# Fourier mixer, ELU FFN and top-1 MoE in one kernel: the shuffles between transform stages moved to DRAM, the last stage respaced

## The chip, the cores and the metric

One core of one Trainium2 chip runs the whole program. The metric is the device time of one execution in microseconds (us), the median of several runs; lower is better. Times on the trace are counted from the span's start.

## The reference, cut to what matters

```python
def _attn_ref(x, w_r, w_i, b_r, b_i):          # x: 8 x 3072 x 256
    X = np.fft.rfft(x, axis=1)
    Yr = X.real @ w_r - X.imag @ w_i + b_r
    Yi = X.real @ w_i + X.imag @ w_r + b_i
    Yr, Yi = softshrink(Yr, 0.01), softshrink(Yi, 0.01)
    return np.fft.irfft(Yr + 1j * Yi, n=3072, axis=1)
def _moe_ref(x, w_in, w_out):                  # 256 -> 2048 -> 256, ELU
    return elu(x @ w_in) @ w_out
def _moe2_ref(x, expert_emb, tau, w1, w2):     # 8 experts, 256 -> 1024 -> 256
    e = argmax of cosine(x, expert_emb) / tau, gate = its softmax value
    return gate * (relu(x @ w1[e]) @ w2[e])
```

`_attn_ref`, `_moe_ref` and `_moe2_ref` follow one another over 24576 tokens.

## The kernel before, in words

**The transform.** For each of 8 batches the length-3072 transform is done in stages, each number held as a high and a low float16 half, so that each product is three matmuls. Stage A (`unit_a`, L168, 16 steps per batch, each with a `split_x` of the input into halves) transforms over 96; stage B (`unit_b`, L198, 24 units) over 32; M (`unit_m` and `unit_m2`, L227 and L258) is the complex 256 x 256 mixing with bias and soft threshold; D (`unit_d`, L268) and E (`unit_e`, L284, 8 blocks of two halves) are the inverse over 32 and over 96. E writes `yT`, the input of one FFN block of 384 tokens.

**The shuffles.** Between A and B, and between D and E, the index that lies on the partitions changes. Both are done by DMA from SBUF to SBUF. A step of A writes two pieces (L191) of 96 KB, from 96 partitions to 4 partitions of `b_in`; in batch 0, six of these go through POOL's queue and the others through SP's. A unit of D writes 128 KB from 128 partitions to 4 partitions of `e_in` (L282). `b_in` and `e_in` hold a whole batch each. B reads all partitions of `b_in`, so its first unit needs the last step of A; E needs the last unit of D in the same way.

**The weights.** `w_in` and `w_out` arrive as float64. Sixteen pieces of 512 KB (`conv_load`, into `raw`, three buffers) are turned into float32 by three integer instructions of DVE (`conv_a` L319, `conv_a2` L328, `conv_b` L334) and split by `conv_c` (ACT, and POOL or DVE). These 64 items stand in the list `fill`; `hook` puts the next one into the program wherever `credit` allows.

**Batch 0** runs alone at the front (L653 to L709): A with some of the conversions (from step `CA`), `CG` items right after it, then B, M, D with the others, one after the other in a loop of 32 turns: turn i issues B of unit i, M of i-2, the second half of M of i-4 and D of i-7. Then the two halves of E's block 0, and the FFN of batch 0 starts.

**Batches 1 to 7** are woven into the FFN of the batch before. The FFN of one batch has NS = 128 steps (8 blocks of 16), each with `ffn1` (L485) and a later `ffn2` (L511). `plan` (L993 to L1013) is a list of (due step, unit), written by hand and sorted: E of the batch's other blocks early, A of the next batch from step 4.25 on, 3.2 steps apart, B from step 57 on, 2.57 steps apart, with M 1.4, its second half 2.3 and D 3.6 steps behind each B; E of the next batch's blocks 0 and 1 from NS-5 on. What is due is issued twice per step. Every engine and DMA queue works in the order of issue.

SP's queue carries the loads of x, both shuffles, the loads of expert weights (`wexp_load`, L434 and L437) and, from `wexp_split`, the write of the split weights to DRAM (L465), which waits for POOL. After batch 7 the routed expert stage follows.

Of the kernel before, what the change touches and what calls it, by code (L numbers as in the profile page):

```python
# [11 lines left out]
F16 = mybir.dt.float16  # L12
F32 = mybir.dt.float32
# [26 lines left out]
XP = 2  # L40
CA, CG, CN, CV = 8, 10, 24, 18
CD = (1, 2, 3, 5, 6, 7)
# [8 lines left out]
def kernel(  # L51
# [25 lines left out]
    keep = ctx.enter_context(tc.tile_pool(name="keep", bufs=1))  # L77
    rows_d = dram.tile([NROW, RW // 2], I32, name="rows_d")
    wexp_d = [dram.tile([NE * 128, 4096], F16, name=f"wexp{i}_d") for i in range(2)]

# [21 lines left out]
    def pool1(name, bufs):  # L102
        return ph1.enter_context(tc.tile_pool(name=name, bufs=bufs))

    spc = pool1("spc", 1)
    big = pool1("big", 1)
    xp = pool1("xp", XP)
    xs = pool1("xs", 3)
    ao = pool1("ao", 3)
    sb = pool1("sb", 3)  # L110
# [39 lines left out]
    def load_x(b, i):  # L150
        src = x[b].rearrange("(n m) c -> n m c", m=N2)[:, 4 * i : 4 * i + 4, :]
        if b == 0:
            if i == 0:
                xpc[0] = big.tile([96, N2, D], F32, tag="e_in", name="x_0")
            t = xpc[0][:, 4 * i : 4 * i + 4, :]
        else:
            t = xp.tile([N1, 4, D], F32, tag="xpc", name="xpc")
        sp.dma_start(out=t, in_=src)
        xpc[b, i] = t
# [8 lines left out]
    def unit_a(b, g):  # L168
        t = xsp.pop((b, g))
        ps = spec_ps()  # L170
        po = ps[:96, :]
        for n, (i, j) in enumerate(((0, 0), (0, 1), (1, 0))):
            pe.matmul(
                po,
                lhsT=f_sb[:, i, :],
                rhs=t[:, j].rearrange("p n c -> p (n c)"),
                start=n == 0,
                stop=n == 2,
            )
        if b or g % 2 == 0:  # L180
            a = ao.tile([96, 2, 2, D], F16, tag="ao", name="ao")
        else:
            a = pre.tile([96, 2, 2, D], F16, tag="ao", name="ao", bufs=5)
        po2 = po.rearrange("p (n c) -> p n c", n=2)
        copy_hi(a[:, :, 0, :], po2, 2.0**-13)
        copy_lo(a[:, :, 1, :], po2, 2.0**-13, a[:, :, 0, :])
        if g == 0:
            b_in[b] = big.tile([128, NJ, 2 * D], F16, tag="b_in", name="b_in")
        for n in range(2):
            n2 = 2 * g + n  # L190
            (sp if b or not n or g % 2 == 0 or g > 12 else pool).dma_start(  # L191
                out=b_in[b][4 * n2 : 4 * n2 + 4, :, :],
                in_=a[:, n].rearrange("p h c -> p (h c)"),
            )

    s_t = {}
    m_t = {}
    def unit_b(b, j):  # L198
        ps = spec_ps()
        for cc in range(2):  # L200
            for n, (h, i) in enumerate(((0, 0), (0, 1), (1, 0))):
                pe.matmul(
                    ps[:, cc * 128 : (cc + 1) * 128],
                    lhsT=b_in[b][:, j, h * D + cc * 128 : h * D + (cc + 1) * 128],
                    rhs=t_sb[:, j, i, :],
                    start=n == 0,
                    stop=n == 2,
                )
# [59 lines left out]
    def unit_d(b, j):  # L268
# [10 lines left out]
        copy_lo(d[:, 1], ps[:, 0:D], 2.0**-12, d[:, 0])  # L279
        if j == 0:  # L280
            e_in[b] = big.tile([96, N2, 2 * D], F16, tag="e_in", name="e_in")
        sp.dma_start(out=e_in[b][4 * j : 4 * j + 4, :, :], in_=d.rearrange("p h c -> p (h c)"))  # L282

    def unit_e(b, blk, cc):  # L284
# [4 lines left out]
        for m in range(4):  # L289
            m2 = 4 * blk + m  # L290
            for n, (h, i) in enumerate(((0, 0), (0, 1), (1, 0))):
                pe.matmul(
                    ps[:, m * 96 : (m + 1) * 96],
                    lhsT=e_in[b][:, m2, h * D + cc * 128 : h * D + (cc + 1) * 128],
                    rhs=e_sb[:, i, :],
                    start=n == 0,
                    stop=n == 2,
                )
# [144 lines left out]
    def wexp_split(c):  # L443
# [3 lines left out]
        if r < 4:  # L447
            cc, q = divmod(r, 2)
            o = wp.tile([128, 2, 512], F16, tag="wh", name="wh", bufs=1)
            ov = o  # L450
# [3 lines left out]
        else:  # L454
            f = 2 * (r - 4)
            o = wp.tile([128, 2, 512], F16, tag="wh", name="wh", bufs=1)
            ov = o.rearrange("p a b -> p (a b)")
# [158 lines left out]
    sp.dma_start(out=f_sb, in_=c_f)  # L616
    for k in range(8):
        load_x(0, k)
    dve.memset(half, 0.5)
# [8 lines left out]
    dve.tensor_copy(base, eoff)  # L628
    with tc.tile_pool(name="pre", bufs=1, side="right") as pre:
        wm = [pre.tile([128, 512], F32, tag=f"wm{ri}", name=f"wm{ri}") for ri in range(2)]  # L630
        emb_sb = pre.tile([NE, D], F32, name="emb_sb")
        conv_load(order[0], pool)
        first = [
# [22 lines left out]
        for i in range(16):  # L656
            step_a(0, i)
            if i % 2:
                first.pop(0)()
            if i in (5, 9):  # L660
                conv_load(order[i // 4])
            if i >= CA:
                credit[0] = 1
                hook()
        sp.dma_start(out=emb_sb, in_=emb)
# [21 lines left out]
        for i in range(NJ + 8):  # L687
# [7 lines left out]
            if 0 <= i - 7 < NJ:  # L695
                unit_d(0, i - 7)
            if i == 0:
                sp.dma_start(out=d_sb, in_=c_d)
            if i == 1:
# [3 lines left out]
            if i >= CV:  # L703
                step_v()
        credit[0] = len(fill)
        hook(len(fill))
# [5 lines left out]
    tp = ctx.enter_context(tc.tile_pool(name="tp", bufs=2, side="right", reuse_waits="tile"))  # L712
    xo = ctx.enter_context(tc.tile_pool(name="xo", bufs=1, side="right", reuse_waits="tile"))
    rt = ctx.enter_context(tc.tile_pool(name="rt", bufs=2, side="right", reuse_waits="tile"))
# [277 lines left out]
    for b in range(B):  # L992
        plan = []  # L993
        for blk, at in zip(range(1, NBLK), (0, 1, 9, 20, 30, 40, 50)):
            if blk > 1 or b == 0:
                for n, u in enumerate(units_e(b, blk)):
                    plan.append((at + 1.5 * n, u))
        if b + 1 < B:
# [3 lines left out]
            for i in range(16):  # L1002
                plan.append((4.25 + 3.2 * i, lambda i=i: step_a(b + 1, i)))
            for j in range(NJ):
                p = 57 + (NS - 12 - 57) * j / (NJ - 1)
                plan.append((p, lambda j=j: unit_b(b + 1, j)))
                plan.append((p + 1.4 + 0.6 * (j in (0, NJ - 1)), lambda j=j: unit_m(b + 1, j)))
                plan.append((p + 2.3, lambda j=j: unit_m2(b + 1, j)))
                plan.append((p + 3.6, lambda j=j: unit_d(b + 1, j)))
            for blk in range(2):  # L1010
                for n, u in enumerate(units_e(b + 1, blk)):
                    plan.append((NS - 5 + 2 * blk + n, u))
        plan.sort(key=lambda p: p[0])  # L1013
# [163 lines left out]
```

## Time and profile before

| | |
|---|---|
| median of 3 runs | 3925.5 us (3922.7 to 3927.98) |
| profiled execution | 3916.23 us, of which span 3914.1 us |
| busy share of the span | PE 94%, PEld 75%, DVE 65%, ACT 58%, POOL 31% |
| SP's hardware DMA queue | 145.66 MB, 21.8% of 16 engines' span |
| HBM read, written | 285.37 MB, 70.03 MB |
| issues of the first shuffle | 250 on SP, 6 on POOL, 96 KB each |
| issues of the second shuffle | 192 on SP, 128 KB each |

In the rows further down, PE is TensorE, PEld its weight load, DVE VectorE, ACT ScalarE, POOL GpSimd, SPq the DMA queue of SyncE. A line of waits names the waiting instruction, what released it, the total, how often and the longest. A line of a timeline gives start, length, engine, line and operation, and in square brackets how long the engine sat idle just before and what ended that. L92 and L95 are the helpers that write the high and the low half.

### The profile page before, as it was taken

The numbers are of one execution on the slowest core, as the hardware profiler recorded it, in microseconds if no ns is written. First come the engines' busy times: TensorE is split into PE (matmuls) and PEld (weight loads), VectorE is DVE, ScalarE is ACT, GpSimd is POOL, SyncE is SP. The second block draws the span as 40 slices with busy tenths as digits, with TensorE's granted clock in tenths as the row PEclk, the third lists the DMA queues.
The fourth block names the chain that finished last, engine by engine and source line by source line (L and its number), as shares of the span: only waits on it lengthen the run. The fifth ranks groups of instructions, "written<-read, shape, count | busy, mean of one in ns | idle before, by whom it ended". The sixth has DMA issues, their size and how long they took to land. (4 is left out here: it accounts for less than half of the span.)

```text
span 3914.1 us, 81873 instructions
## 1 busy us (share of the span) xinstructions
PE 3697.7 (94%) x32108; PEld 2930.5 (75%) x32108; DVE 2551.1 (65%) x5647; ACT 2267.9 (58%) x4749; POOL 1215.7 (31%) x1529
## 2 busy tenths in 40 slices
PE   3699999999999999999999999999999999999998
PEld 2577777777777777777777777777788899999997
DVE  4676767767677777767677776766665555555554
ACT  3586677668667766866876686677732222222221
POOL 2412223223222222322322232233234444344443
PEclk6899999999999999999999999999999999999999
DMA  6342233224223322422332242210234345533332
GB/s 158 79 68 40 37 60 62 38 43 76 39 38 60 60 37 44 76 38 38 61 60 37 45 77 37 39 46 31 72 97 125 105 115 166 156 77 94 102 90 64
DMA packets 274220, 272.72 MB, mean 70 GB/s; under 512 B 169091, under 2 KB 235354, under 8 KB 265512
## 3 DMA queue, kind: packets, MB, share of 16 engines
q1 hardware_dynamic: 221944, 145.66, 21.8%
q0 software_dynamic: 51888, 121.83, 9.8%
q8 instruction: 251, 4.11, 0.5%
q14 instruction: 137, 1.12, 0.1%
HBM read 285.37 MB, written 70.03 MB: 91 GB/s over the span
## 5 line engine op out<-in xcount | busy, mean ns | idle before, releaser
L511 PE MATMUL ps_a<-wout,ghl 128*128 128x264 f16 x9216 | 1200.3, 276 | 6.6 <-DVE ghl L95 6.1
L485 PE MATMUL ps_h<-yT,win 128*128 128x384 f16 x6144 | 1167.4, 326 | 6.2 <-DVE do L95 3.4
L511 PEld LDWEIGHTS <-ghl 128*128 128x128 f16 x9216 | 890.0, 98 | 209.7 <-DVE ghl L95 11.2
L501 DVE SCALAR_TENSOR_TENSOR g<-e,ps_h 128x384 f32<-128x384 f32 x1024 | 564.7, 552 | 570.7 <-ACT e L498 567.7
L485 PEld LDWEIGHTS <-win 128*128 128x128 f16 x6144 | 596.1, 98 | 314.6 <-issue 10.3
L497 ACT ACTIVATE e<-ps_h 128x384 f32<-128x384 f32 x1024 | 494.0, 482 | 371.7 <-PE ps_h L485 358.6
L913 ACT ACTIVATE r<-ps_h 128x512 f32<-128x512 f32 (+1 forms) x440 | 244.7, 556 | 796.1 <-PE ps_h L907 773.4
L498 ACT ACTIVATE e<-e,top 128x384 f32<-128x384 f32 x1024 | 629.8, 615 | 33.2
L95 DVE SCALAR_TENSOR_TENSOR ghl<-g,ghl 128x768 f16<-128x768 f32 x512 | 510.4, 997 | 85.6 <-ACT ghl L92 85.6
L928 PE MATMUL ps_a<-wbuf,g 128*128 128x256 f16 x4776 | 554.7, 273 | 2.5 <-DVE g L915 1.4
L907 PE MATMUL ps_h<-xt,wbuf 128*128 128x256 f16 (+1 forms) x5280 | 555.5, 262 | 0.0
L907 PEld LDWEIGHTS <-wbuf 128*128 128x128 f16 x5280 | 477.7, 98 | 49.3
L928 PEld LDWEIGHTS <-g 128*128 128x128 f16 x4776 | 464.9, 98 | 57.3 <-DVE g L915 2.5
L606 POOL DMA_INDIRECT rows_d<-row,pi x192 | 203.2, 1059 | 747.8 <-DMA rows_d<-row,pi 309.0
L92 ACT ACTIVATE ghl<-g 128x768 f16<-128x768 f32 x512 | 423.5, 827 | 0.6 <-DVE g L501 0.6
L946 POOL DMA_INDIRECT out_dram<-o,mt x199 | 208.4, 1047 | 518.6 <-DVE o L938 303.4
L914 DVE CAST g<-r 128x512 f16<-128x512 f32 (+1 forms) x440 | 178.5, 406 | 284.2 <-ACT r L913 281.9
L601 POOL COPY row<-gt 128x1 f32<-128x1 f32 x192 | 26.9, 179 | 1083.8 <-DVE gt L597 1083.8
L915 DVE TENSOR_TENSOR g<-r,g 128x512 f16<-128x512 f32 (+1 forms) x440 | 283.0, 643 | 15.1
L241 PE MATMUL ps_h<-wmix,s_t 128*128 128x256 f16 x2106 | 269.5, 274 | 10.4 <-DVE s_t L95 6.4
L241 PEld LDWEIGHTS <-s_t 128*128 128x128 f16 x2256 | 218.8, 99 | 66.1 <-DVE s_t L95 14.0
L938 DVE TENSOR_SCALAR o<-ps_a,mt 128x256 f32<-128x256 f32 x199 | 96.3, 484 | 176.1 <-PE ps_a L928 170.5
(178 smaller groups left out, 3397.7 us busy)
## 6 DMA issues: line engine op xcount, KB each, us to landing
e_in<-do SPq DMA_DIRECT2D x192, 128.0 KB
b_in<-ao SPq DMA_DIRECT2D x250, 96.0 KB
xpc<-in_x_dram SPq DMA_DIRECT2D x56, 384.0 KB
wl<-in_moe_w_dram SPq DMA_DIRECT2D x64, 256.0 KB
wexp_d<-wh SPq DMA_DIRECT2D x64, 256.0 KB
raw<-in_moe_w_in_dram SPq DMA_DIRECT2D x8, 512.0 KB
raw<-in_moe_w_out_dram SPq DMA_DIRECT2D x7, 512.0 KB
out_dram<-o,mt POOLq DMA_INDIRECT x199
```

Source lines behind the costliest of these rows:

```text
L92: act.activation(out=o, in_=i, func=AF.Copy, scale=k)
L95: dve.scalar_tensor_tensor(out=o, in0=i, scalar=k, in1=hi, op0=ALU.mult, op1=ALU.subtract)
L241: pe.matmul(ps[:, 0:D], lhsT=st, rhs=wmix[:, ri, i, cc, :], start=n == 0, stop=n == 11)
L485: pe.matmul(ps[:, 0:BLK], lhsT=win[:, i, cc, f * 128 : (f + 1) * 128], rhs=y[:, h, cc, :], start=n == 0, stop=n == 5,)
L497: act.activation(out=e, in_=ps[:, 0:BLK], func=AF.Exp, scale=2.0**-19)
L498: act.activation(out=e, in_=e, func=AF.Relu, scale=-(2.0**19), bias=top)
L501: dve.scalar_tensor_tensor(out=g, in0=e, scalar=-1.0, in1=ps[:, 0:BLK], op0=ALU.mult, op1=ALU.max)
L511: pe.matmul(a_t[b, blk][t][:, 0:WOC], lhsT=g[:, h, f % 2, t * 128 : (t + 1) * 128], rhs=wout[:, f, i, :], start=f == 0 and n == 0, stop=f ...
L907: pe.matmul(ps[:, j, 0:n], lhsT=w[:, c : c + 128], rhs=xt[:, 2 * h + cc, :], start=m == 0, stop=m == 5)
L913: act.activation(out=r[:, :, 0:n], in_=ps[:, :, 0:n], func=AF.Relu, scale=2.0**-9)
L915: dve.tensor_tensor(out=g[:, q, 1, :, 0:n], in0=r[:, :, 0:n], in1=g[:, q, 0, :, 0:n], op=ALU.subtract)
L928: pe.matmul(ps[:, 0:D], lhsT=g[:, f // 2, h, f % 2, t * 128 : (t + 1) * 128], rhs=w[:, c : c + 256], start=m == 0, stop=m == 23,)
```

## The change

Both shuffles go through DRAM. A step of A makes one DMA of 192 KB from 96 partitions into `b_d` (two of them, by batch parity); B reads it back in six pieces of 512 KB, each for four units, into three buffers: the first three right after A, the others two pieces ahead of their use. A unit of D writes 128 KB into `e_d`; E reads it back in eight pieces of 384 KB into two buffers. The input of batch 0 moves to the pool `pre`. In batch 0, no conversion is issued during A, `CG` falls from 10 to 4 and the rest is spread over 30 turns in place of 24; the weight loads on POOL's queue are issued one per step from step 0; `raw` is loaded on SP at steps 6, 8 and 10. In `plan`, E of block `blk` is due at step 16*blk - 11 (in the last batch as before, but for the first blocks), with its load 6 steps ahead; A begins at 3.4 with 3.0 steps between; B begins at 55; M, its second half and D lie 1.6, 2.8 and 4.6 steps behind B; only block 0 of the next batch's E is done at the end, from NS-2.6. `wh` and `xf` get a second buffer, `ao` has five for all batches.

```diff
-CA, CG, CN, CV = 8, 10, 24, 18
+JC = 4
+CG, CN, CV = 4, 30, 18
...
+    b_d = [dram.tile([128, NJ, 2 * D], F16, name=f"b{i}_d") for i in range(2)]
+    e_d = [dram.tile([96, N2, 2 * D], F16, name=f"e{i}_d") for i in range(2)]
...
-    big = pool1("big", 1)
+    bc = pool1("bc", 3)
+    ec = pool1("ec", 2)
-    ao = pool1("ao", 3)
+    ao = pool1("ao", 5)
...
-                xpc[0] = big.tile([96, N2, D], F32, tag="e_in", name="x_0")
+                xpc[0] = pre.tile([96, N2, D], F32, name="x_0")
...
-        for n in range(2):
-            n2 = 2 * g + n
-            (sp if b or not n or g % 2 == 0 or g > 12 else pool).dma_start(
-                out=b_in[b][4 * n2 : 4 * n2 + 4, :, :],
-                in_=a[:, n].rearrange("p h c -> p (h c)"),
-            )
+        sp.dma_start(
+            out=b_d[b % 2][8 * g : 8 * g + 8].rearrange("(n q) j x -> (q j) n x", n=2),
+            in_=a.rearrange("p n h c -> p n (h c)"),
+        )
+    def load_b(b, c):
+        if c < NJ // JC:
+            b_in[b, c] = bc.tile([128, JC, 2 * D], F16, tag="b_in", name="b_in")
+            sp.dma_start(out=b_in[b, c], in_=b_d[b % 2][:, c * JC : (c + 1) * JC, :])
+    def load_e(b, blk):
+        e_in[b, blk] = ec.tile([96, 4, 2 * D], F16, tag="e_in", name="e_in")
+        sp.dma_start(out=e_in[b, blk], in_=e_d[b % 2][:, 4 * blk : 4 * blk + 4, :])
...
-        sp.dma_start(out=e_in[b][4 * j : 4 * j + 4, :, :], in_=d.rearrange("p h c -> p (h c)"))
+        sp.dma_start(
+            out=e_d[b % 2][4 * j : 4 * j + 4].rearrange("q m x -> (q m) x"), in_=d.rearrange("p h c -> p (h c)")
+        )
...
-            o = wp.tile([128, 2, 512], F16, tag="wh", name="wh", bufs=1)
+            o = wp.tile([128, 2, 512], F16, tag="wh", name="wh")
...
-        conv_load(order[0], pool)
...
-            if i % 2:
+            if first:
                 first.pop(0)()
-            if i in (5, 9):
-                conv_load(order[i // 4])
-            if i >= CA:
-                credit[0] = 1
-                hook()
+            if i in (6, 8, 10):
+                conv_load(order[i // 2 - 3])
+        for c in range(3):
+            load_b(0, c)
+        sp.dma_start(out=d_sb, in_=c_d)
...
-            if i == 0:
-                sp.dma_start(out=d_sb, in_=c_d)
+            if i % JC == 1 and i > JC:
+                load_b(0, i // JC + 2)
...
+        load_e(0, 0)
+        load_e(0, 1)
         credit[0] = len(fill)
...
-    xo = ctx.enter_context(tc.tile_pool(name="xo", bufs=1, side="right", reuse_waits="tile"))
+    xo = ctx.enter_context(tc.tile_pool(name="xo", bufs=2, side="right", reuse_waits="tile"))
...
-        for blk, at in zip(range(1, NBLK), (0, 1, 9, 20, 30, 40, 50)):
-            if blk > 1 or b == 0:
-                for n, u in enumerate(units_e(b, blk)):
-                    plan.append((at + 1.5 * n, u))
+        for blk in range(1, NBLK):
+            at = (2, 4, 9, 20, 30, 40, 50)[blk - 1] if b + 1 == B else 16 * blk - 11
+            if blk > 1:
+                plan.append((max(0, at - 6), lambda blk=blk: load_e(b, blk)))
+            for n, u in enumerate(units_e(b, blk)):
+                plan.append((at + 1.5 * n, u))
...
-                plan.append((4.25 + 3.2 * i, lambda i=i: step_a(b + 1, i)))
+                plan.append((3.4 + 3.0 * i, lambda i=i: step_a(b + 1, i)))
+            for c in range(3):
+                plan.append((51.6, lambda c=c: load_b(b + 1, c)))
             for j in range(NJ):
-                p = 57 + (NS - 12 - 57) * j / (NJ - 1)
+                p = 55 + (NS - 14 - 55) * j / (NJ - 1)
                 plan.append((p, lambda j=j: unit_b(b + 1, j)))
-                plan.append((p + 1.4 + 0.6 * (j in (0, NJ - 1)), lambda j=j: unit_m(b + 1, j)))
-                plan.append((p + 2.3, lambda j=j: unit_m2(b + 1, j)))
-                plan.append((p + 3.6, lambda j=j: unit_d(b + 1, j)))
+                plan.append((p + 1.6 + 0.6 * (j in (0, NJ - 1)), lambda j=j: unit_m(b + 1, j)))
+                plan.append((p + 2.8, lambda j=j: unit_m2(b + 1, j)))
+                plan.append((p + 4.6, lambda j=j: unit_d(b + 1, j)))
+                if j % JC == 1 and j > JC:
+                    plan.append((p + 0.2, lambda j=j: load_b(b + 1, j // JC + 2)))
             for blk in range(2):
-                for n, u in enumerate(units_e(b + 1, blk)):
-                    plan.append((NS - 5 + 2 * blk + n, u))
+                plan.append((NS - 6.2, lambda blk=blk: load_e(b + 1, blk)))
+            for n, u in enumerate(units_e(b + 1, 0)):
+                plan.append((NS - 2.6 + n, u))
```

## Rows read from the trace of the kernel before

**Rows 1.** Stretches: us, PE, PEld, DVE, ACT, POOL busy (instructions), granted clock, DMA share, GB/s

```profile
0.00:10.00 10.00, 3.65 (x9) 1.81 (x10) 4.05 (x28) 4.75 (x7) 1.60 (x7) 1.00 0.80 210
...
10.00:20.00 10.00, 7.75 (x20) 3.49 (x19) 6.07 (x10) 4.75 (x9) 4.24 (x6) 1.00 1.06 214
...
0.00:50.00 50.00, 19.92 (x45) 8.38 (x46) 19.32 (x52) 17.10 (x30) 9.88 (x20) 0.70 0.74 147
50.00:100.00 50.00, 18.06 (x134) 13.12 (x133) 25.37 (x47) 16.26 (x34) 14.72 (x16) 0.58 0.63 168
...
518.80:859.00 340.20, 328.14 (x2736) 247.11 (x2736) 242.38 (x552) 245.92 (x525) 89.15 (x128) 0.99 0.28 50
```

**Rows 2.** Waits of PE, 235 to 2690 us: total us, times, longest us

```profile
PE ps_h L272 <- DVE mm L265: 35.7, 56, 1.5
PE ps_h L292 <- DMA e_in<-do: 17.0, 7, 2.6
PE ps_h L202 <- DMA wl<-in_moe_w_dram: 13.7, 5, 2.9
PE ps_h L272 <- ACT mm L264: 11.3, 20, 1.0
...
PE ps_h L202 <- DMA b_in<-ao: 5.3, 2, 2.8
```

**Rows 3.** Timeline of ACT, 0 to 86 us

```profile
5.54 1.15 ACT L92 ACTIVATE xsp<-x 96x512 f16<-96x512 f32 x2 [3.51 <-DMA x<-in_x_dram]
...
31.46 0.59 ACT L92 ACTIVATE ao<-ps_a 96x512 f16<-96x512 f32 x1 [15.75 <-DMA b_in<-ao]
```

**Rows 4.** Waits of all engines, whole span

```profile
ACT ao L92 <- DMA b_in<-ao: 39.5, 5, 15.7
...
ACT do L92 <- DMA e_in<-do: 17.3, 10, 3.9
```

**Rows 5.** Timeline of SP's queue, 0 to 110 us

```profile
1.21 3.90 SPq L158 DMA_DIRECT2D x<-in_x_dram  x8
9.35 23.15 SPq L191 DMA_DIRECT2D b_in<-ao  x9
...
64.42 10.05 SPq L191 DMA_DIRECT2D b_in<-ao  x8
```

**Rows 6.** Timeline of PE, from 0 us and from 500 us

```profile
6.21 4.29 PE L173 MATMUL ps_h<-xsp,f_sb 96*96 96x512 f16 x9 [6.21 <-ACT xsp L92]
...
15.64 2.17 PE L173 MATMUL ps_h<-xsp,f_sb 96*96 96x512 f16 x6
...
83.09 2.08 PE L202 MATMUL ps_h<-t_sb,b_in 128*128 128x128 f16 x18 [18.90 <-DMA tri<-in_c_tri_dram]
...
186.14 2.08 PE L292 MATMUL ps_h<-e_sb,e_in 96*128 96x96 f16 x24 [7.48 <-DMA e_in<-do]
...
518.82 1.12 PE L292 MATMUL ps_h<-e_sb,e_in 96*128 96x96 f16 x12 [2.51 <-DMA e_in<-do]
```

**Rows 7.** Waits of SP's queue: first row whole span, second 1880 to 2220 us

```profile
SPq L872 <- DMA rows_d<-zrow: 9.0, 8, 4.1
...
SPq L465 <- POOL wh L464: 20.7, 6, 7.8
```

**Rows 8.** Groups of DVE, 83 to 180 us: busy us, mean ns, idle before

```profile
L334 DVE SCALAR_TENSOR_TENSOR c_t<-raw,msk,c_t 128x512 int32<-128x512 int32 x12 | 11.8, 986 | 0.0
...
L328 DVE SCALAR_TENSOR_TENSOR c_t<-raw,msk,c_t 128x512 int32<-128x512 int32 x12 | 9.3, 772 | 0.1
L319 DVE TENSOR_SCALAR c_t<-raw 128x512 int32<-128x512 int32 x12 | 8.1, 677 | 8.5 <-DMA raw<-in_moe_w_out_dram 8.5
...
L95 DVE SCALAR_TENSOR_TENSOR do<-ps_h,do 128x256 f16<-128x256 f32 x12 | 5.0, 420 | 9.7 <-ACT do L92 9.7
```

**Rows 9.** Timeline of DVE: the last unit of D of batch 0

```profile
176.07 0.42 DVE L95 SCALAR_TENSOR_TENSOR do<-ps_a,do 128x256 f16<-128x256 f32 x1 [1.51 <-ACT do L92]
```

**Rows 10.** Groups that write yT, whole span: ns min/median/max

```profile
L92 ACT ACTIVATE yT<-ps_h x128: 467/471/492, 187.4 to 2693.3; 128x384 f16<-128x384 f32 x128
L95 DVE SCALAR_TENSOR_TENSOR yT<-ps_h,yT x128: 543/551/560, 187.9 to 2694.1; 128x384 f16<-128x384 f32 x128
```

More of the change, by code (lines that the diff above doesn't have):

```diff
@@ L179, in unit_a @@
             )
[L180 to L183, printed above, removed]
+        a = ao.tile([96, 2, 2, D], F16, tag="ao", name="ao")
         po2 = po.rearrange("p (n c) -> p n c", n=2)
@@ L186, in unit_a @@
         copy_lo(a[:, :, 1, :], po2, 2.0**-13, a[:, :, 0, :])
-        if g == 0:
-            b_in[b] = big.tile([128, NJ, 2 * D], F16, tag="b_in", name="b_in")
-        for n in range(2):
-            n2 = 2 * g + n
-            (sp if b or not n or g % 2 == 0 or g > 12 else pool).dma_start(
-                out=b_in[b][4 * n2 : 4 * n2 + 4, :, :],
-                in_=a[:, n].rearrange("p h c -> p (h c)"),
-            )
+        sp.dma_start(
[9 more added lines that the diff above has]
+        sp.dma_start(out=e_in[b, blk], in_=e_d[b % 2][:, 4 * blk : 4 * blk + 4, :])
     s_t = {}
@@ L203, in unit_b @@
                     ps[:, cc * 128 : (cc + 1) * 128],
-                    lhsT=b_in[b][:, j, h * D + cc * 128 : h * D + (cc + 1) * 128],
+                    lhsT=b_in[b, j // JC][:, j % JC, h * D + cc * 128 : h * D + (cc + 1) * 128],
                     rhs=t_sb[:, j, i, :],
@@ L279, in unit_d @@
         copy_lo(d[:, 1], ps[:, 0:D], 2.0**-12, d[:, 0])
-        if j == 0:
-            e_in[b] = big.tile([96, N2, 2 * D], F16, tag="e_in", name="e_in")
-        sp.dma_start(out=e_in[b][4 * j : 4 * j + 4, :, :], in_=d.rearrange("p h c -> p (h c)"))
+        sp.dma_start(
+            out=e_d[b % 2][4 * j : 4 * j + 4].rearrange("q m x -> (q m) x"), in_=d.rearrange("p h c -> p (h c)")
+        )
     def unit_e(b, blk, cc):
@@ L289, in unit_e @@
         for m in range(4):
-            m2 = 4 * blk + m
             for n, (h, i) in enumerate(((0, 0), (0, 1), (1, 0))):
@@ L293, in unit_e @@
                     ps[:, m * 96 : (m + 1) * 96],
-                    lhsT=e_in[b][:, m2, h * D + cc * 128 : h * D + (cc + 1) * 128],
+                    lhsT=e_in[b, blk][:, m, h * D + cc * 128 : h * D + (cc + 1) * 128],
                     rhs=e_sb[:, i, :],
@@ L455, in wexp_split @@
             f = 2 * (r - 4)
-            o = wp.tile([128, 2, 512], F16, tag="wh", name="wh", bufs=1)
+            o = wp.tile([128, 2, 512], F16, tag="wh", name="wh")
             ov = o.rearrange("p a b -> p (a b)")
@@ L616 @@
     sp.dma_start(out=f_sb, in_=c_f)
-    for k in range(8):
-        load_x(0, k)
     dve.memset(half, 0.5)
@@ L629 @@
     with tc.tile_pool(name="pre", bufs=1, side="right") as pre:
+        for k in range(8):
+            load_x(0, k)
         wm = [pre.tile([128, 512], F32, tag=f"wm{ri}", name=f"wm{ri}") for ri in range(2)]
         emb_sb = pre.tile([NE, D], F32, name="emb_sb")
-        conv_load(order[0], pool)
         first = [
```

## The prediction

> **What bounds the kernel now.** I read the stretches first. From 235 us on PE is nearly always at work: the second batch's stretch of 340.20 us has PE busy for 328.14 [rows 1], so 12.1 us of each batch is left. In the first 100 us PE works for 38 us only [rows 1]. So there are two places to win: the front, where batch 0 runs alone, and the small gaps of each batch.
>
> The front, in the timelines. ACT's first split of x starts at 5.54 us, and nine steps of A run on PE from 6.21 to 17.81 us, 1.29 us each; then ACT stands still for 15.75 us until a DMA of `b_in` has left its buffer, and altogether 39.5 us in this way [rows 3, 4, 6]. B begins at 83.09 us [rows 6]. Over those 74 us SP and POOL issued the 32 pieces of the first shuffle, from 9.35 us to after 64.42 us [rows 5]: 2.3 us a piece of 96 KB, 42 GB/s, while the queues as a whole had moved 210 GB/s in the first 20 us [rows 1]. What is slow is this shape of write, 4 partitions at a time, not the amount. The second shuffle has the same shape: ACT waits 17.3 us on it in ten units of D [rows 4]. D's last copy ends at 176.5 us [rows 9], and E starts at 186.1 us after a DMA wait [rows 6].
>
> The batches, in the waits of PE from 235 to 2690 us [rows 2]: D waits on the second half of M for 35.7 + 11.3 = 47.0 us; B's first units on a DMA for 13.7 + 5.3 = 19.0 us (the `wl` named is a neighbour in the queue; the unit needs `b_in`); E on `e_in` for 17.0 us. Sum 83.0 us, which fits 7 x 12.1 = 84 us from the stretch.
>
> **The change part by part: the front.** The sum is made against the profiled execution, 3916.2 us.
>
> Stage A: without the stuck buffers its 16 steps at 1.29 us end at 6.2 + 20.6 = 26.8 us. No conversion is in it now. Then the last write has to land in DRAM and the first 512 KB to come back. The trace shows no such pair. A write of 132 KB to DRAM was waited for at most 4.1 us [rows 7]; 384 KB of x came 4.3 us after their issue (1.21 to 5.54) [rows 3, 5], 5.8 us for 512 KB at that rate. That gives 36.7 us at the early end. The late end is by bytes: x 3.1, twiddles and weights 2.4, three pieces of raw 1.6, the writes 3.1, together 10.3 MB, 49 us at the 210 GB/s of the first stretch, and 5.8 us for the read: 55 us. I take 46 for the start of B, in the middle, because both limits are near each other: 37 us won.
>
> The Trainium skill ("DMA: Bandwidth & Descriptors", Anatomy of one DMA, there for POOL's path) speaks against this part: it puts about 2.0 us of fixed cost on each DMA, mostly the receipt of the write, heaviest when HBM is the target. An estimate by its formula for the two hops is 2.0 + 0.5 and 2.0 + 1.2 us, 5.7 in place of the 9.9 above; B would start some 4 us sooner, and the sum would be 3806. No run here shows either hop alone.
>
> B, M and D: 83.1 to 176.5 us is 93.4 us, and DVE is the bound there (no idle before L334 and L328) [rows 8]. Of the 64 conversion items 8 + 10 were issued before B, now 4; 14 items, 3.5 pieces of weight, come in. Each costs DVE 986 + 772 + 677 ns [rows 8]: +8.5 us, with no cover. What goes is the wait on `e_in` (17.3 us on ACT [rows 4]; DVE stood before `do` for 9.7 us in half of the units [rows 8]), as a write no longer lands on 4 partitions. I take 12 us of it: 93.4 + 8.5 - 12 = 90 us; ends 85 (all of it) and 102 (none).
>
> To E: now 9.6 us. A write at 4.1 and a read of 384 KB at 4.3: 8.4 us; ends 4 and 10. So E starts at 46 + 90 + 8.4 = 144.4 in place of 186.1 us: **-42 us**; ends 125.7 (-60) and 167 (-19).
>
> **The batches.** A step of `plan` is 340.2 / 128 = 2.66 us.
>
> D: from M to D the plan had 2.2 steps, now 3.0; 0.8 steps are 2.1 us, more than the longest wait of 1.5 us [rows 2]. Against it: the stretch where B, M and D run now also takes four blocks of E, eight halves of 0.47 us on ACT and 0.55 on DVE [rows 10], which delay some. I take 42 of the 47.0 us. Ends 47 and 0 (the new units put back what the spacing gives).
>
> B: from the last step of A to B were 4.75 steps, now 6.6, 17.6 us. Needed are some 2 us of copies, 4.1 and 5.8: 12. I take 17 of 19.0; ends 19 and 10.
>
> E: from the last D to E were 3.4 steps, now 6.8, 18 us; needed 2 + 4.1 + 4.3. But the loads of E stand in SP's queue behind the write of `wexp_split` of step 120, and SP waits for POOL up to 7.8 us there [rows 7]: issued at 121.8, they could start at 123.4 and land at 125.0, just before E at 125.4. So 15 of 17.0; ends 17 and 5.
>
> Together **-74 us**; ends -83 and -15.
>
> Costed at nothing: the other loads of `load_b` and `load_e` (at 5.8 or 4.3 us each, issued 16 us and more ahead, covered by FFN; without that cover up to 7 x 10 x 5 us); the loads of x and expert weights behind them in SP's queue, which has about as many issues a batch as before (78 for 80); the loads moved on POOL's queue, where nothing else stands in stage A; the second buffers of `wh` and `xf`, as no wait of PE is put down to either; the pitch of A, whose units are the same work; in the last batch the load of block 3, which SP has to hold until block 1 is done, 5 steps before its use. What comes after 2850 us is the same. When the gaps are gone, FFN on PE is what comes next.
>
> Sum: 3916.2 - 42 - 74 = 3800. The median stands 9.3 us above the profiled execution, so **3810 us**.
>
> **The rivals.**
>
> *The front is bound by bytes.* PE stood still with the DMA engines at 0.63 to 0.74 of their time [rows 1], and the change moves the shuffle twice. If 147 GB/s [rows 1] is what such a mix gives, 10.8 MB take 73 us, B gains 10, the stage after it loses the 8.5 and nothing is left: 3925.5 - 76 = 3850. Against it: the same engines moved 210 GB/s when few shuffle writes were in flight. Chance 0.13. Beside it stands a rule of the Trainium skill ("DMA: Bandwidth & Descriptors", Why a DMA increments its semaphore by 16 and not by 1): a DMA runs on the largest number of engines up to 16 that divides the slowest dimension of both sides, so 4 before and 16 now; by that rule this rival falls. No view here lists the engines.
>
> *D goes on waiting.* The extra E units take DVE and ACT exactly where M's second half stands, and the 47 us stay: 3810 + 42 = 3852. For it: ACT and DVE are busy for 0.72 of a batch's stretch [rows 1], and M's chain crosses both several times. Against: 2.1 us more against a longest wait of 1.5. Chance 0.12.
>
> *Slower: the round trip through DRAM becomes the wait.* Its place is before the first B and the first E of each batch. With L us a hop, a chain takes 2L + 2 of 17.6 to 18 us, so from L = 8 on all 14 chains stall by 2L - 15.8, and the front's E starts at 116.8 + 4L. Against -42 for D, the sum is (4L - 69) - 42 - 36 + 14 x (2L - 15.8), over zero from L = 11.5; at 12.5 it is about +30, 3957. For it: SP works in order and waits for POOL [rows 7]. Against: the longest hops seen are 4.1 and 4.3 us. Chance 0.03.
>
> *Nothing to measure:* what PE wins is lost on ACT and DVE. Chance 0.02.
>
> **How the numbers follow.** The forecast has 0.70. A difference of 0.2%, 8 us, is about what a measurement of this kernel can tell from none; all three cases above it lie far outside. The range starts at 3780 (front at -60 with -83, 3782) and reaches 3860, past the two rivals of 0.13 and 0.12; the low ends of both parts together (-34, 3892) are left out. Faster 0.95, within 0.2% 0.02, slower 0.03.
>
> **What would show each step.** B's first matmul near 46 us and E's near 144 us, with no `ao` waiting on a DMA, would show the front right; B near 70 us its byte rival. Waits of PE at L272 under 10 us in total show the spacing right; waits at L202 and L292 under 6 us the chains. A stretch of one batch should fall by 10 to 11 us. If E's waits grow to several us a batch, the queue behind `wexp_split` was undercounted; a wait of PE at L485 on `yT` at the batch's first step would be the price of E's block 0 coming at NS-2.6 in place of NS-5.

## The result and the profile after

The changed kernel takes 3777.8 us (median of 4 runs, 3774.64 to 3779.74); in the same set the kernel before takes 3926.74 us (3922.7 to 3929.47). The ratio is 0.9621, 95% interval 0.9604 to 0.9637: 3.8% less. Forecast were 3810 us with a range from 3780 to 3860. The direction and both places of the gain were right; the gain was larger than forecast, and the time lies 2 us below the range.

The profiled execution took 3777.07 us, its span is 3775.3 us. Three marks cut the span into the parts of the prediction: the start of E of batch 0, the first matmul of the expert stage, and the end.

| part, us | before | after | difference | forecast |
|---|---|---|---|---|
| start to E of batch 0 (front) | 186.1 | 133.5 | -52.6 | -42 |
| E of batch 0 to the expert stage (batches) | 2664.8 | 2575.4 | -89.4 | -74 |
| expert stage | 1063.1 | 1066.2 | +3.1 | 0 |

The expert stage takes between 1061 and 1066 us in the profiles of all the kernels below, so its +3.1 us asks for no explanation.

The page of the changed kernel: busy time of the engines and the traffic with HBM.

```profile
PE 3670.7 (97%) x32108; PEld 2924.0 (77%) x32108; DVE 2540.2 (67%) x5647; ACT 2266.4 (60%) x4749; POOL 1204.6 (32%) x1522
...
HBM read 335.70 MB, written 120.36 MB: 121 GB/s over the span
```

PE has 97% of the span, and the reads and writes of HBM together are 121 GB/s on average, far below the rates of the front that follow: over the whole kernel no byte limit is in sight. The front has to be read by itself.

The stretches of the changed kernel, with the columns of [rows 1]: the first three belong to the front, the fourth is one batch, the fifth reaches from E of batch 0 to the expert stage.

```profile
0.00:50.00 50.00, 22.72 (x97) 12.50 (x98) 28.13 (x72) 24.20 (x45) 7.91 (x17) 0.76 0.89 270
...
0.00:40.00 40.00, 16.73 (x48) 7.54 (x48) 23.46 (x59) 19.78 (x35) 6.76 (x16) 0.80 0.90 257
...
40.00:50.00 10.00, 5.99 (x49) 4.96 (x50) 4.68 (x14) 4.42 (x10) 1.15 (x1) 0.60 0.86 322
...
803.73:1133.22 329.49, 324.76 (x2738) 246.28 (x2737) 245.45 (x555) 248.15 (x529) 88.44 (x129) 1.00 0.24 72
...
133.60:2709.00 2575.40, 2538.34 (x21300) 1919.82 (x21301) 1870.55 (x4245) 1944.48 (x4108) 696.83 (x1015) 1.00 0.24 71
```

The stretch that answers to the fifth, in the kernel before:

```profile
186.10:2850.90 2664.80, 2557.57 (x21300) 1922.16 (x21301) 1877.65 (x4245) 1943.45 (x4108) 706.54 (x1015) 1.00 0.27 51
```

The first 50 us now move 270 GB/s, where they moved 147 [rows 1]. One batch takes 329.5 us instead of 340.2 [rows 1], and PE is idle in it for 4.7 us instead of 12.1. In the whole stretch PE is idle for 37.1 us instead of 107.2, and busy for 2538.3 us instead of 2557.6 with the same matmuls.

Timeline of PE: the first unit of B and the first of E, which answer to [rows 6].

```profile
44.01 2.10 PE L208 MATMUL ps_h<-t_sb,b_in 128*128 128x128 f16 x18 [9.11 <-DMA b_in<-b_d]
...
133.50 2.10 PE L297 MATMUL ps_h<-e_sb,e_in 96*128 96x96 f16 x24 [2.12 <-DVE row L725]
```

Timeline of ACT, which answers to [rows 3], and of SP's queue, which answers to [rows 5].

```profile
23.95 0.59 ACT L95 ACTIVATE ao<-ps_a 96x512 f16<-96x512 f32 x1 [10.28 <-DMA b_d<-ao]
```

```profile
32.49 4.99 SPq L188 DMA_DIRECT2D b_d<-ao  x5
...
40.01 1.29 SPq L196 DMA_DIRECT2D b_in<-b_d  x3
```

B starts at 44.01 us, E at 133.50. The last writes of the first shuffle have been issued by 37.5 us, the reading back is issued at 40.01, and B starts 4.0 us later. So the way through DRAM took some 2.5 + 4.0 = 6.5 us. ACT still stood 10.3 us for a buffer of A, from 13.7 to 23.95 us.

Waits of PE in the changed kernel, 200 to 2600 us, with the columns of [rows 2].

```profile
PE ps_h L490 <- DVE g L506: 9.1, 15, 0.8
PE ps_a L516 <- DVE ghl L98: 6.2, 20, 0.6
PE ps_h L208 <- DVE mt L253: 5.6, 7, 0.8
PE ps_h L177 <- DVE xsp L98: 4.2, 6, 0.7
PE ps_h L177 <- ACT xsp L95: 2.9, 6, 0.5
PE ps_h L297 <- DMA e_in<-e_d: 0.8, 3, 0.4
```

The three kinds of wait that made 83.0 us [rows 2] are gone but for 0.8 us of E: no line names D (now L278), and B (L208) waits for no DMA. What is left is small, and nearly all of it is waits on DVE and ACT.

### The profile page after: what moved, and what is told of

Its sections match the earlier page's. It is cut to its first block, busy times and chain, and to the rows that moved or that the text cites. A ratio compares the mean times of both kernels' runs of the same rounds, so it can differ in the third digit from the quotient of the medians.

```text
span 3775.3 us, 81848 instructions
## 1 busy us (share of the span) xinstructions
PE 3670.7 (97%) x32108; PEld 2924.0 (77%) x32108; DVE 2540.2 (67%) x5647; ACT 2266.4 (60%) x4749; POOL 1204.6 (32%) x1522
## 5 line engine op out<-in xcount | busy, mean ns | idle before, releaser
L490 PE MATMUL ps_h<-yT,win 128*128 128x384 f16 x6144 | 1162.1, 326 | 9.1 <-DVE g L506 9.1
L490 PEld LDWEIGHTS <-win 128*128 128x128 f16 x6144 | 595.9, 98 | 308.3 <-issue 13.4
L98 DVE SCALAR_TENSOR_TENSOR ghl<-g,ghl 128x768 f16<-128x768 f32 x512 | 500.2, 977 | 83.8 <-ACT ghl L95 81.4
L556 POOL TENSOR_TENSOR row<-xf,row 128x256 f16<-128x256 f32 x192 | 166.0, 864 | 249.8 <-ACT row L555 248.9
```

What stands on the lines that cost most here:

```text
L98: dve.scalar_tensor_tensor(out=o, in0=i, scalar=k, in1=hi, op0=ALU.mult, op1=ALU.subtract)
L490: pe.matmul(ps[:, 0:BLK], lhsT=win[:, i, cc, f * 128 : (f + 1) * 128], rhs=y[:, h, cc, :], start=n == 0, stop=n == 5,)
```

## The experiments

Each set of runs had the kernel before beside it: 3913.42 us in the first set (7 runs; with the old spacing, E early, the first shuffle in SBUF, and the conversions), 3914.62 in the second (7; with the kernel before spaced anew, four outer rows, and late twiddles) and 3920.41 in the third (9; with three buffers of x, and the last two kernels). Ratios are against these.

**The old spacing in the changed kernel.** Is it the spacing that took D's waits away, and is a stop of PE worth more than its listed time?

```diff
-plan.append((p + 1.6 + 0.6 * (j in (0, NJ - 1)), lambda j=j: unit_m(b + 1, j)))
-plan.append((p + 2.8, lambda j=j: unit_m2(b + 1, j)))
-plan.append((p + 4.6, lambda j=j: unit_d(b + 1, j)))
+plan.append((p + 1.4 + 0.6 * (j in (0, NJ - 1)), lambda j=j: unit_m(b + 1, j)))
+plan.append((p + 2.3, lambda j=j: unit_m2(b + 1, j)))
+plan.append((p + 3.6, lambda j=j: unit_d(b + 1, j)))
```

> The changed kernel with only the offsets of M, its second half and D behind B put back to 1.4, 2.3 and 3.6 steps. Theory L (a wait of PE is worth what the list of waits says): D's 47.0 us come back, 3778 + 47 = 3825, a batch 328.8 + 6.7 = 335.5 us. Theory T (each stop costs 0.16 us more than listed, because the last matmul before it is drawn 0.16 us longer than the spacing of its successors, 1.14 against 0.98 us): 76 stops more by 0.16, +59, 3837, a batch 337.2 us. Third: the spacing is not what removed the waits, 3778.

Measured: 3824.81 us, ratio 0.9777 (0.9761 to 0.9794), 47 us more than the changed kernel's 3777.8; in the profiles the batches took 41.8 us more. Waits of PE in this kernel, 200 to 2600 us, and the stretch of its batches.

```profile
PE ps_h L278 <- DVE mm L271: 17.9, 37, 0.8
PE ps_h L278 <- DVE g L506: 12.7, 7, 1.8
PE ps_h L278 <- ACT mm L270: 12.2, 7, 1.7
```

```profile
133.70:2750.90 2617.20, 2548.10 (x21301) 1919.49 (x21302) 1859.85 (x4246) 1939.94 (x4109) 694.62 (x1015) 1.00 0.23 70
```

D's waits are back: 17.9 + 12.7 + 12.2 = 42.8 us in 51 stops. So the new offsets remove them, and the way through DRAM alone does not. The edit moves M, its second half and D; which of the three does it was not tried apart. Against the changed kernel's stretch, PE is idle 69.1 us instead of 37.1 (+32.0) and busy 2548.1 us instead of 2538.3 (+9.8) with the same matmuls. So stops show up in the busy time as well. The total does not decide between the readings: the median is the 3825 us of theory L, and 42.8 us of listed waits against 41.8 us in the batches fit it too. Only the split into idle and busy time speaks for theory T, whose 3837 us were not reached: D's stops are 51 and not 76 [rows 2], and other waits went. In all, the stretch has 43 stops more; at 0.16 us they make 6.9 of the 9.8 us.

Why a stop lengthens the busy time is seen in the timeline of PE in the kernel before, around one of E's waits at 858.77 us (the first row, from 519.74 us, is for later).

```profile
519.74 2.18 PE L511 MATMUL ps_a<-wout,ghl 128*128 128x264 f16 x9
...
855.65 1.14 PE L485 MATMUL ps_h<-yT,win 128*128 128x384 f16 x6
856.62 1.18 PE L511 MATMUL ps_a<-wout,ghl 128*128 128x264 f16 x9
857.63 1.14 PE L485 MATMUL ps_h<-yT,win 128*128 128x384 f16 x6
861.06 0.67 PE L292 MATMUL ps_h<-e_sb,e_in 96*128 96x96 f16 x12 [2.29 <-DMA e_in<-do]
```

A group of L485 is drawn 1.14 us long, but undisturbed the next group starts 0.97 us after it: the ends of pipelined matmuls overlap. After a stop they don't. From 857.63 to 861.06 are 3.43 us where 0.98 would have done; 2.45 us are lost, and 2.29 are listed. That is 0.16 us a stop that no wait shows. PE's listed stops between E of batch 0 and the expert stage number 156 before and 65 after: 91 x 0.16 = 14.6 us. The other kernels below bear the direction out: PE is busy in this stretch, with the same matmuls, for 2537 to 2540 us where it has 59 to 65 stops, for 2548 to 2554 us where it has 93 to 108, and for 2558 us in the kernel before.

**E as early as in the last batch.** Does spreading E over the batch win anything?

```diff
-at = (2, 4, 9, 20, 30, 40, 50)[blk - 1] if b + 1 == B else 16 * blk - 11
+at = (2, 4, 9, 20, 30, 40, 50)[blk - 1]
```

> The changed kernel with E of all batches due early, at steps 2, 4, 9, 20, 30, 40 and 50 as in its last batch, in place of spread. Theories L and T: E's place costs nothing by itself, 3778 within 4 us, a batch 328.8 us. Rival S (the 4.5 us a batch that went beyond the listed idle time went through the spreading of E, because ACT was crowded in the first half of a batch): 3778 + 7 x 4 = 3806, a batch 333 us.

Measured: 3763.11 us, ratio 0.962 (0.9604 to 0.9636), below the changed kernel's 3777.8; in the profiles the batches took 9.3 us less. None of the readings had expected a gain. The ratio by itself shows none against the changed kernel's 0.9621, as the kernel before was 13 us faster in this set; both versions stand in one set further down. The stretch of its batches:

```profile
132.90:2699.00 2566.10, 2537.43 (x21301) 1921.82 (x21302) 1839.78 (x4246) 1946.80 (x4109) 700.68 (x1015) 1.00 0.23 71
```

PE is idle 28.7 us instead of 37.1. Spreading E costs the batches some 9 us here: the idea that it buys room was refuted. That its blocks take DVE and ACT where B, M and D need them fits the waits that went (PE at L490 for `g`, 9.1 us, at L208 for `mt`, 5.6 us), but wasn't tested apart.

**The new spacing in the kernel before.** What does the spacing bring without the way through DRAM?

```diff
-plan.append((4.25 + 3.2 * i, lambda i=i: step_a(b + 1, i)))
+plan.append((3.4 + 3.0 * i, lambda i=i: step_a(b + 1, i)))
...
-p = 57 + (NS - 12 - 57) * j / (NJ - 1)
+p = 55 + (NS - 14 - 55) * j / (NJ - 1)
...
-plan.append((p + 2.3, lambda j=j: unit_m2(b + 1, j)))
-plan.append((p + 3.6, lambda j=j: unit_d(b + 1, j)))
+plan.append((p + 2.8, lambda j=j: unit_m2(b + 1, j)))
+plan.append((p + 4.6, lambda j=j: unit_d(b + 1, j)))
```

> The kernel before (shuffles in SBUF, E early, front as it was) with only the hand-written steps of the woven stages changed as in the change: A from 3.4 at 3.0, B from 55, M, its second half and D 1.6, 2.8 and 4.6 behind. Theory T with the schedule as the cause: D's, B's and E's waits all go (E gets one step more, 2.7 us against a wait of 2.5): 3927 - 83 - 90 stops x 0.16 = 3830, a batch 329 us. Theory L: 3927 - 83 = 3844. Rival (the waits of B and E need the DRAM shuffles): only D's go, 3927 - 47 to 59, 3868 to 3880.

Measured: 3869.62 us, ratio 0.9884 (0.9867 to 0.99). The batches took 2621.0 us, 43.8 less than before. Their stretch, and waits of PE, 220 to 2630 us:

```profile
182.70:2803.70 2621.00, 2553.52 (x21300) 1922.30 (x21301) 1851.73 (x4245) 1943.04 (x4109) 693.54 (x1015) 1.00 0.28 52
```

```profile
PE ps_h L292 <- DMA e_in<-do: 13.9, 7, 2.1
PE ps_a L511 <- DVE ghl L95: 12.0, 22, 0.8
PE ps_h L485 <- DVE g L501: 9.7, 9, 1.7
```

D's waits and B's on a DMA are gone, without the way through DRAM; E's stay at 13.9 us [rows 2: 17.0], and new small ones on DVE came up. So PE is idle only 39.7 us less, though 66 us of listed waits went. The total fell where the third reading had put it, 3868 to 3880, but not for its reason: B's waits went too. So the 89.4 us of the batches split, along the way over these kernels, into the spacing (-43.8, from before to this kernel), the rest of the change (-54.9, from this kernel to the one with E early), and the spreading of E (+9.3). The rest holds both shuffles, the queue order, the second buffers and the new place of E's first blocks, which were not all tried apart; the next run undoes the first shuffle by itself.

**The first shuffle back between SBUF and SBUF**, all on SP's queue.

```diff
-bc = pool1("bc", 3)
+bc = pool1("bc", 1)
...
-sp.dma_start(
-    out=b_d[b % 2][8 * g : 8 * g + 8].rearrange("(n q) j x -> (q j) n x", n=2),
-    in_=a.rearrange("p n h c -> p n (h c)"),
-)
+for n in range(2):
+    n2 = 2 * g + n
+    sp.dma_start(out=b_in[b][4 * n2 : 4 * n2 + 4, :, :], in_=a[:, n].rearrange("p h c -> p (h c)"))
...
```

> The changed kernel with the first shuffle back in SBUF: two pieces of 96 KB a step onto 4 partitions, all on SP; the second shuffle stays in DRAM. Theory P (the four-partition pieces are what held stage A): 32 pieces at 2.3 us, B at about 83 us, 39 us later; the batches lose nothing, as 6.6 steps (17 us) lie between the last A and B and the landing took 8 us: 3778 + 39 = 3817. Rival (bytes bound the front): B at 40 to 55 us, 3778 to 3789.

Measured: 3853.26 us, ratio 0.9852 (0.9836 to 0.9869). PE's first unit of B, the stretch of the batches, then ACT's waits from 0 to 180 us and from 480 to 2450 us:

```profile
75.78 2.08 PE L210 MATMUL ps_h<-t_sb,b_in 128*128 128x128 f16 x18 [21.61 <-DMA d_sb<-in_c_d_dram]
```

```profile
165.40:2780.80 2615.40, 2550.96 (x21300) 1918.42 (x21301) 1866.12 (x4245) 1944.04 (x4109) 685.98 (x1015) 1.00 0.26 61
```

```profile
ACT ao L95 <- DMA b_in<-ao: 33.9, 10, 15.5
...
ACT xsp L95 <- DMA xpc<-in_x_dram: 22.9, 12, 3.5
```

B starts 31.8 us later, where 39 were expected: the front had stood for this way of writing, not for the amount of work. A miss is in the batches: they took 40.0 us more, where none was expected. ACT now waits 22.9 us for x, whose loads stand behind the slow pieces in SP's queue.

**Three buffers of x in that kernel**, so that x can be loaded earlier.

```diff
-XP = 2
+XP = 3
...
-ao = pool1("ao", 5)
+ao = pool1("ao", 4)
```

> The first shuffle in SBUF as in the fourth experiment, with a third buffer for the input pieces of the woven stage A (and four for ao in place of five). Theory Q (the four-partition pieces hold up the loads of x, which stand behind them in the same queue; ACT then waits for x and with it the FFN): most of the 40 us that the batches lost come back, FFN stretch 2580 to 2590 us, total 3810 to 3820. If they come back not at all, the loss has another way: 3847.

Measured: 3863.94 us (3842.04 to 3878.08), ratio 0.987 (0.9847 to 0.9893). ACT's waits for x fell from 22.9 us to none, but in the profile only 9.8 of the 40.0 us came back in the batches (2605.6 us), and that profile is of the fastest of four runs, which spread over 36 us. By the median this kernel is 10.7 us slower than the one with two buffers, and with four buffers of `ao` in place of five B starts 3.3 us later, at 79.04 us. So the late x accounts for a quarter of the loss at most. Waits of PE in this kernel, 480 to 2450 us:

```profile
PE ps_a L518 <- DVE ghl L98: 11.2, 24, 1.4
PE ps_h L492 <- DVE g L508: 7.9, 13, 0.8
PE ps_h L299 <- DMA e_in<-e_d: 5.0, 7, 2.0
...
PE ps_h L299 <- DVE xsp L98: 2.4, 1, 2.4
```

E's reading back, behind the same pieces in the queue, is late by 5.0 us in all; the rest stays spread over small waits on DVE, whose cause stays open.

**Four outer rows, but in DRAM.** Is a write of four rows slow because of its four rows, or because it lands on four SBUF partitions? The rows of `b_d` and `e_d` get a gap, and each write covers four of them, as many and as large as the pieces of the kernel before.

```diff
-b_d = [dram.tile([128, NJ, 2 * D], F16, name=f"b{i}_d") for i in range(2)]
-e_d = [dram.tile([96, N2, 2 * D], F16, name=f"e{i}_d") for i in range(2)]
+b_d = [dram.tile([128, NJ + 1, 2 * D], F16, name=f"b{i}_d") for i in range(2)]
+e_d = [dram.tile([96, N2 + 1, 2 * D], F16, name=f"e{i}_d") for i in range(2)]
...
+        out=b_d[b % 2][4 * n2 : 4 * n2 + 4, 0:NJ, :],
...
+        out=e_d[b % 2][4 * j : 4 * j + 4, 0:N2, :], in_=d.rearrange("p h c -> p (h c)")
```

> The changed kernel with both shuffles written to DRAM in pieces whose outer dimension on the target is 4 rows (96 KB each for the first, 128 KB for the second), as the old ones in SBUF were; the rows of the DRAM buffers are padded by one so that the four stay apart. Theory K (a piece with four outer rows is slow wherever it lands): stage A takes 32 x 2.3 us again, B at about 83 to 88 us, D waits for its buffers as before (17 us), 3778 + 50 to 60 = 3833. Theory N (it is slow because it lands on four partitions of SBUF): B at 44 to 50 us, 3778 to 3785.

Measured: 3798.42 us, ratio 0.97 (0.9684 to 0.9716). PE's first unit of B, and ACT's waits up to 180 us:

```profile
64.33 2.10 PE L210 MATMUL ps_h<-t_sb,b_in 128*128 128x128 f16 x18 [20.21 <-DMA b_in<-b_d]
```

```profile
ACT ao L95 <- DMA b_d<-ao: 25.4, 11, 11.8
```

Neither reading held alone. B starts 20.3 us later than in the changed kernel, E 24.6, and the batches are unchanged (2575.1 us instead of 2575.4). Of the 31.8 us that the SBUF shuffle costs B, four outer rows in twice as many pieces are 20.3, and landing on four SBUF partitions the other 11.5, or more, as only the way through DRAM has the reading back in it. The edit changes the number of pieces together with their rows; the two weren't tried apart.

**Conversions in A again**, as before the change: 18 items before B (eight in A, ten right after it) in place of 4.

```diff
-CG, CN, CV = 4, 30, 18
+CG, CN, CV = 10, 24, 18
...
+            if i >= 8:
+                credit[0] = 1
+                hook()
```

> The changed kernel with the conversions placed as before: one item per step of A from step 8, ten right after A, the others over 24 turns. By the prediction's term the stage of B, M and D gets 8.5 us shorter; but the first raw piece is issued at 26.8 us and DVE, which works in order, would stand until it has landed, some 6 to 9 us in stage A. Net 3778 within 6 us, E of batch 0 between 128 and 139 us. If conversions in A are free as they were thought before: 3769.

Measured: 3777.44 us, ratio 0.9651 (0.9635 to 0.9667). PE's first units of B and of E:

```profile
50.98 2.10 PE L208 MATMUL ps_h<-t_sb,b_in 128*128 128x128 f16 x18 [8.81 <-DMA b_in<-b_d]
...
137.47 2.10 PE L297 MATMUL ps_h<-e_sb,e_in 96*128 96x96 f16 x24 [3.49 <-DMA e_in<-e_d]
```

B starts 7.0 us later and E 4.0 us later: the stage between them becomes 3.0 us shorter, 86.5 instead of 89.5. The 14 items cost the stage of B, M and D 3 us and not 8.5, and A some 7 us, of which DVE stood 3.1 us for the first piece of `raw`. Moving them out of A is worth 4 us to E in the profiles; the median of the whole kernel doesn't tell it from none.

**Three of four twiddle pieces later**, each after a reading back, so that 1.2 MB less go before B.

```diff
-        for k in range(4):
+        for k in range(1):
...
+            sp.dma_start(out=t_sb[:, 6 * c + 6 : 6 * c + 12], in_=c_t[:, 6 * c + 6 : 6 * c + 12])
```

> The changed kernel with three of the four pieces of the twiddle factors of B (1.2 MB) loaded on SP, one behind each of the first three reads of the first shuffle, in place of on POOL's queue in stage A. If the start of B is set by the bytes moved until then (10 MB by 44 us): B 5 us sooner, 3773. If it is set by the pace of A and the landing of its last write: 3778.

Measured: 3769.14 us, ratio 0.9627 (0.9611 to 0.9643). PE's first unit of B:

```profile
40.59 2.10 PE L208 MATMUL ps_h<-t_sb,b_in 128*128 128x128 f16 x18 [8.90 <-DMA b_in<-b_d]
```

B starts 3.4 us sooner, and E of batch 0 2.9 us. By the profiles the rest of what the time fell lies mostly behind the batches, in an expert stage that is 4.5 us shorter though nothing in it was changed. 1.2 MB are 4.4 us at the 270 GB/s of the first 50 us, so most of the bytes taken away turn into time, as they should if bytes bound the new front.

**The changed kernel once more, and with E early and late twiddles together.** The second is the two edits shown above in one kernel.

> The changed kernel itself once more, on the same chip as the next two. Its ratio to the kernel before was 0.9621 when the kernel before took 3927 us; if the 13 us by which the kernel before was faster in the two later sets of runs belong to the chip, this one takes 3765 to 3778.

> The changed kernel with E of all batches early and three pieces of twiddles late, the two edits that were each faster. If they add up: the FFN stretch 9.5 us shorter, the front 3 us; 12 to 15 us below the changed kernel of this set. If what they won was the chip's: no difference.

Measured, in one set: 3777.45 us, ratio 0.9639 (0.9625 to 0.9653), and 3766.0 us, ratio 0.9615 (0.9599 to 0.9631). The stretch of the second's batches, and its first unit of B:

```profile
130.40:2699.30 2568.90, 2537.22 (x21301) 1921.33 (x21302) 1839.25 (x4245) 1946.72 (x4109) 700.85 (x1015) 1.00 0.24 71
```

```profile
40.09 2.10 PE L208 MATMUL ps_h<-t_sb,b_in 128*128 128x128 f16 x18 [8.79 <-DMA b_in<-b_d]
```

The median is 11.5 us below the changed kernel of its set, a little under the 12 to 15 expected, and the slowest of its five runs (3774.14 us) lies below the fastest of the changed kernel's (3775.24). By the profiles of this set the batches are 7.5 us shorter and E of batch 0 starts 3.3 us sooner; alone the two edits had 9.3 and 2.9. So by these stretches they about add up. The changed kernel repeats to 0.4 us between the sets, while the kernel before ran at 3913.4, 3914.6, 3920.4 and 3926.7 us in four sets.

## Why the prediction was right, and where it fell short

The miss against the profiled execution is 3800 - 3777 = 23 us: 10.6 from the front and 15.4 from the batches, less the 3.1 us by which the expert stage grew. The other 9 us are the offset between median and profile.

**Start of B: right, in part by luck.** 44.0 us came, 46 were forecast. The late end, by bytes, has the mechanism, with another rate: its 10.3 MB are what was moved by 40.0 us, when the reading back was issued (257 GB/s over these 40 us in place of 210), and the read took 4.0 us more. The late twiddles support it. But that end was 55 us in the forecast, and 46 came near only because it lay in the middle between this and an early end that was out of reach: ACT did stand for a buffer (10.3 us), which the prediction had ruled out. The whole way through DRAM took 6.5 us; the forecast's 9.9 was too long. The estimate by the Trainium skill ("DMA: Bandwidth & Descriptors", Anatomy of one DMA) was 5.7 for it, which is nearer.

**B, M and D: the conversion term was too large.** 83.6 us came (44.0 to 127.65, the end of D's last copy), 90 were forecast. The term of 8.5 us measured 3.0 in the kernel with conversions in A. With it, 93.4 + 3.0 - 12 = 84.4, so the 12 us for `e_in` fits: ACT's `do` has no listed wait on a DMA any more. The 14 items were priced at their full length, since DVE was taken for the bound of this stage, with no idle before two of their three operations [rows 8]. The stage before, then after, shows that it was not:

```profile
83.09:176.49 93.40, 67.85 (x640) 54.38 (x640) 70.49 (x160) 49.62 (x138) 45.31 (x55) 0.85 0.45 109
...
44.01:127.65 83.64, 64.43 (x646) 52.10 (x647) 72.77 (x167) 51.84 (x144) 51.92 (x58) 0.93 0.51 165
```

DVE was idle for 22.9 of the 93.4 us before. The operations on `c_t` from `raw` took it 29.2 us for 36 in the stage before and 30.8 us for 43 after, so seven more of them added 1.5 us and not their full length; two others ran behind the stage. **To E:** 5.85 us came, 8.4 were forecast, and by the profile the last to arrive was DVE, not the DMA.

**The batches: the failed step is the price of a stop.** The prediction read 83.0 us of waits, checked them against 7 x 12.1 us of PE's idle time, and set its most favourable end, -83, by that; a stop of PE was worth what the list shows, and its effect on the busy time was put at nothing. PE's idle time between E and the expert stage did fall by 70.1 us (107.2 to 37.1), near the 74 forecast: the three waits went but for 0.8 us, and some 12 us of other small waits took part of it back. But PE's busy time fell too, from 2557.6 to 2538.3 us, by 19.3, with the same matmuls, and no term had that. Of these, an estimated 14.6 us are the 91 stops that went, at the 0.16 us read from one of them in the timeline; that busy time falls with the number of stops is shown by the other kernels. For the other 4.7 us the best candidate is the granted clock after a long stop: in the kernel before, the first stretch here follows E's wait of 2.51 us [rows 6], and the others follow waits of 2.69, 2.81 and 2.71 us before a first unit of B.

```profile
519.00:522.00 3.00, 3.00 (x22) 2.21 (x21) 1.25 (x4) 0.49 (x1) 0.00 (x0) 0.50 0.37 129
...
324.50:327.50 3.00, 3.00 (x13) 1.66 (x11) 0.94 (x7) 0.74 (x3) 0.00 (x0) 0.50 0.12 41
1007.00:1010.00 3.00, 2.33 (x14) 1.84 (x15) 0.95 (x4) 0.38 (x1) 0.48 (x1) 0.50 0.28 94
2372.50:2375.50 3.00, 3.00 (x18) 2.00 (x16) 1.30 (x7) 0.61 (x2) 0.00 (x0) 0.50 0.28 91
```

The granted clock was 0.50, the lower level of 1.2 GHz, in all four. The group of nine matmuls at 519.74 us in the timeline above took 2.18 us, where the same group takes 1.18 at 856.62, and all of it counts as busy. Between E of batch 0 and the expert stage the clock stood at this level for 18.7 us before and for 6.7 us after, by the traces' rows of the clock. At half the rate the difference is worth 6.0 us at most, an estimate, so it can hold the 4.7 us; no run varied the clock alone.

**D, B and E by themselves** went as forecast in direction, and further: D won all of its 47.0 us, B all 19.0 on a DMA (6.1 us on DVE came in its place), E 16.2 of 17.0. The queue behind the expert weights did not hold E up (0.8 us).

**The offset.** The 9.3 us by which the median of before lay over its profiled run were carried to the changed kernel, whose median lies 0.7 us over its own. They were not a property to carry: in three other sets the kernel before itself stood 5 to 12 us lower than the 3925.5 shown then.

**The rivals.** The byte rival named the right limit and the wrong rate: not 147 GB/s but 270, as the pieces with four rows were what had kept the rate down (over the first 50 us 187 GB/s with four rows in DRAM, 163 with four partitions of SBUF). The rule of the Trainium skill ("DMA: Bandwidth & Descriptors", Why a DMA increments its semaphore by 16 and not by 1) by which this rival would fall agrees with that: four outer rows, brought back in DRAM with twice as many pieces, cost B 20.3 us. Landing on four SBUF partitions costs at least 11.5 more, which that rule leaves out. That D goes on waiting fell: it took the old spacing to bring the 42.8 us back. The slower rival needed 11.5 us for a hop; in the front 4.0 was the longer one, and in the batches E's waits of 0.8 us leave no room for it. That the E units press on ACT and DVE, the ground of the second rival, fits the 9.3 us that the spreading of E costs the batches.

## What to carry to other kernels

Price a stop of TensorE by the starts of its neighbours in the timeline and not by its listed wait: by the estimate above, the 91 stops that went here were worth 14.6 us more than their listed sum. When a shuffle is slow, look at how many outer rows each DMA writes and where it lands, and ask what stands behind it in its queue, before adding buffers. A change made of several edits can hold one that costs, as the spread E does here, so undo them one by one.

## What was not expected of the hardware

The queues moved 270 GB/s over the first 50 us and 322 GB/s from 40 to 50 us, where the front before had reached 214 GB/s in its first 20 us [rows 1] and 271 from 80 to 90 us, after the slow pieces. Going through DRAM (192 KB out, 512 KB in) took 6.5 us and was the shorter way: the same shuffle from SBUF to SBUF, four partitions at a time, started B 31.8 us later. And the same pieces cost the batches 40.0 us, of which 9.8 at most came back with the 22.9 us of waits for x; what the others are stays open.
